# A transformer block on one core: halves at the head, five more rows turned by DMA, means spread through DRAM, all Q/K pairs as seven products

## The chip, the cores and the metric

The kernel runs on one core of a Trainium2 chip. Its engines work side by side, each through its own row of instructions in order: TensorE (PE; its weight loads are listed as PEld), VectorE (DVE), ScalarE (ACT), GpSimd (POOL) and SyncE (SP), whose queue issues all DMAs here. The metric is the device time of one execution in microseconds (us); a kernel's time is the median of its runs.

## The reference, cut to what matters

```python
h  = x + attention(layernorm(x) @ wqkv) @ wo
h2 = h + (gelu(layernorm(h) @ w_gate) * (layernorm(h) @ w_up)) @ w_down
```

x is 2048 x 512, float32. Attention has 32 heads of 16 columns; each position sees eight positions, itself and seven earlier ones at a distance of 2, 4, ... 14, with a softmax over these eight. The feed-forward width is 1792. Layernorm has no learned scale.

## The kernel before

**Tiling.** Four chunks c of 512 tokens, in each four rows j of 128 tokens; 512 columns are four blocks of 128. Tokens are laid on partitions so that the distance of 2 becomes a distance of 1. A float32 product runs as three products in a reduced format: each operand is split into a high part and the rest (`split`: a cast, usually on ScalarE, for `xTh`, `hTh`, `wh`; a subtraction on DVE or POOL for `xTl`, `hTl`, `wl`), and high x high, high x low and low x high are added up. One projection of a row is thus 12 matmuls of 128x512.

**Chunk 0's start.** `WARM` transposes of nothing run on TensorE first (`warm_ps`). `prep0(j)` takes row j's statistics on DVE (`bn_stats`, L585), centres all 512 columns on ScalarE (L587), turns four blocks on TensorE (`tp_x`, L469), and evicts and splits them. `project(c, s, j)` makes k (s=1), q (s=0) or v (s=2); the variance is applied when the sum is evicted.

**Chunks 1 to 3.** x comes transposed from DRAM (`xc`) and is centred there by a tile `mb`, in which the row means lie on every partition: `stats(c)` spreads the means by four TensorE transposes (L629) and a ScalarE copy (L633), for c = 1 and 2. (Chunk 3's x is turned by DMA instead.) `project_pair(c, p)` makes q and k of two rows as seven half-size products in place of eight (L766, into `qka`, `qkb`, `qkc`), with sums of x rows (`sums`: `xS`, `xSl`) and of weights (`weight_sums`: `wsa`, `wsb`, `wT`), which cost DVE and POOL additions and the evictions `qkvt` on DVE (L781). That is 42 matmuls for 48. The pairs in `PLAIN`, here chunk 1's first, take the 48.

**Attention.** `attention(c)` works on four groups of eight heads. k and v go to DRAM and come back shifted (`kw`, `vw`). DVE multiplies (`pk`, L870), reduces (`lg`, L873), multiplies by v (`pv`, L912) and adds up in halves (L917, L919, shared with POOL) to `o_0` to `o_3`. o is turned for the next matmul by DMA (`crossed`: ScalarE copy, DMA transpose, ScalarE copy, then the split) or by TensorE (`tp_o`).

**Tail and feed-forward.** `tail(c)` multiplies by wo (`wo_0` to `wo_3`, one sum per row), adds x (`h`), normalises each row (`norm`: statistics and the last step on DVE, the power on POOL; `xhat_h`) and turns it: by four TensorE transposes `tp_h` with `transpose4`, or, for chunks in `CROSS_H`, by DMA with `crossed` (tile `a_h`). `ffn(c)` runs 14 steps of 128 columns: `pg` and `pu`, the gelu, the product, and `acc` for w_down. Chunks 2 and 3 share one joint feed-forward stage (`last_two`, `joint`, `last_sums`) that again saves products by sums: `combine(j)` makes sums of chunk 2's and 3's hT (`tt`, `tth`, `ttl`) straight from the PSUM bank of `tp_h`, `pa` and `pc` are its accumulators, `jt` their copies on ScalarE.

**Order.** Every operation is added to a plan. `schedule` puts them in order with a list scheduler, which reads one rank per operation from the table `RANKS`; the table `SWAPS` says which operations run on their second engine (DVE or POOL for `either`, ScalarE or DVE for `evict`).

Of the kernel before, what the change touches and what calls it, by code (L numbers as in the profile page):

```python
# [16 lines left out]
P = 128  # L17
D = 512
# [16 lines left out]
WARM = 36  # L35
ONDVE = (1,)
YIELD = 20000
# [6 lines left out]
FINE = (1,)  # L44
FIRST = [("x", 0), (1, 0), (1, 1), ("x", 1), (1, 2), (1, 3), ("x", 2), ("x", 3)] + [(0, k) for k in range(KD)]
# [7 lines left out]
PLAIN = ((1, 0),)  # L53
# [7 lines left out]
CROSS_H = (1, 2)  # L61
RANKS = (
# [186 lines left out]
class Tile:  # L249


    def __init__(self, plan, pool, tag, shape, dtype, name):
        self.make = lambda: pool.tile(shape, dtype, tag=tag, name=name, bufs=1)
        self.ap = None
        self.parts = {}
        self.users = set()
        self.before = plan.slots.get((id(pool), tag))
        plan.slots[id(pool), tag] = self

    def __call__(self):  # L260
# [1282 lines left out]
```

## Time and profile before

| | |
|---|---|
| median of 3 runs | 625.03 us (624.29 to 625.63) |
| profiled execution, its own time | 624.23 us |
| its span, first to last instruction | 622.4 us |
| granted TensorE clock, mean | 1.000 |
| busy: PE, DVE, ACT, POOL | 614.1, 541.4, 426.7, 422.6 us |
| DMA bytes | 153.19 MB, 246 GB/s over the span |

The profile is of one execution. A row of the timeline has its start and length in us, the engine, the source line, the operation, output<-inputs, the shape and how many instructions the row holds; in square brackets stands how long the engine idled before and who released it. A matmul's end is modelled, so that rows on TensorE overlap: the distance of two starts tells the cadence.

### The profile page before, as it was taken

What the parts mean: (1) busy time and instruction counts of PE and PEld (TensorE: products, weight loads), DVE (VectorE), ACT (ScalarE), POOL (GpSimd) and SP (SyncE); (2) the same over time, 40 slices, a digit from 0 to 9 for tenths busy, and PEclk for the clock granted to TensorE, in tenths of its full rate; (3) what the DMA queues carried; (4) which work ended last, traced back from release to release, by engine and by line L of the source; (5) the groups of instructions that cost most, each with busy time, mean ns of one, the idle gap of its engine ahead of it and who ended that gap; (6) DMA issues with size and microseconds to landing.
All of it is one profiled execution on the core that took longest, in us unless ns stands there. A gap on an engine that the chain in (4) does not pass through costs nothing.

```text
span 622.4 us, 8450 instructions
## 1 busy us (share of the span) xinstructions
PE 614.1 (99%) x2728; PEld 503.9 (81%) x2728; DVE 541.4 (87%) x614; ACT 426.7 (69%) x743; POOL 422.6 (68%) x373
## 2 busy tenths in 40 slices
PE   8999999999999999999999999999999999999997
PEld 7888887878888888888888888877768878888885
DVE  4789999898999899999899999979849888768994
ACT  5797587547645666997767767978856666658751
POOL 4999888655899898573577773546475736578751
PEclk9999999999999999999999999999999999999999
DMA  8766688599969887999979897984756555639973
GB/s 299 265 213 250 199 257 265 165 334 309 327 216 323 255 239 225 323 317 355 325 276 314 294 295 214 240 255 108 222 180 216 181 184 194 219 110 309 250 220 102
DMA packets 101084, 153.19 MB, mean 246 GB/s; under 512 B 42016, under 2 KB 55072, under 8 KB 100656
## 3 DMA queue, kind: packets, MB, share of 16 engines
q1 hardware_dynamic: 101040, 152.65, 77.2%
q8 instruction: 21, 0.34, 0.2%
q14 instruction: 23, 0.19, 0.1%
HBM read 107.48 MB, written 36.23 MB: 231 GB/s over the span
## 4 chain that ended last, share of the span: by engine, by line
PE 88%; DMA 4%; DVE 3%; ACT 2%; issue 1%; POOL 1%; SPq 0%; DVEq 0%; ACTq 0%; POOLq 0%
PE pg L544 12%; PE pu L544 12%; PE qkv L544 10%; PE dn L1315 10%; PE pa L1197 8%; PE wo L544 7%; PE pc L1197 5%; PE acc L1006 4%; PE acc L1004 4%; PE acc L1005 4%; PE qka L766 3%; DMA fraw<-in_wffn_dram 2%; PE pg L1419 2%; PE qkv L537 2%; PE pu L1419 1%; PE qkc L766 1%
## 5 line engine op out<-in xcount | busy, mean ns | idle before, releaser
L917 POOL TENSOR_TENSOR pv<-pv 128x1024 f32<-128x1024 f32 (+1 forms) x44 | 84.8, 1931 | 19.5 <-DVE pv L912 18.6
L870 DVE TENSOR_TENSOR pk<-kw,qp 128x2048 f32<-128x2048 f32 x32 | 72.9, 2278 | 1.6 <-ACT qp L863 0.8
L873 DVE TENSOR_REDUCE lg<-pk 128x128 f32<-128x2048 f32 x32 | 72.8, 2278 | 0.5
L912 DVE TENSOR_TENSOR pv<-vw,qp 128x2048 f32<-128x2048 f32 x32 | 72.6, 2281 | 0.6
L544 PE MATMUL pg<-hTh,gu 128*128 128x512 f32 x224 | 59.9, 389 | 0.0
L544 PE MATMUL pu<-hTh,gu 128*128 128x512 f32 x224 | 59.9, 389 | 0.0
L544 PEld LDWEIGHTS pg<-hTh,gu 128*128 128x128 f32 x224 | 42.0, 188 | 8.9 <-ACT hTh L457 0.2
L544 PEld LDWEIGHTS pu<-hTh,gu 128*128 128x128 f32 x224 | 42.0, 188 | 8.7
L1004 PE MATMUL acc<-dnh,gh 128*128 128x512 f32 x112 | 43.6, 389 | 0.0
L1005 PE MATMUL acc<-dnl,gh 128*128 128x512 f32 x112 | 43.6, 389 | 0.0
L1006 PE MATMUL acc<-dnh,gl 128*128 128x512 f32 x112 | 43.6, 389 | 0.0
L458 POOL TENSOR_TENSOR gl<-g,gh 128x512 fp32r<-128x512 f32 x21 | 27.8, 1323 | 9.6 <-ACT gh L457 9.6
L458 POOL TENSOR_TENSOR gu<-fraw,gu 128x512 fp32r<-128x512 f32 x22 | 29.7, 1358 | 6.6 <-ACT gu L457 6.6
L1197 PE MATMUL pa<-tt,jh 128*128 128x512 f32 x112 | 30.3, 392 | 0.3 <-ACT jh L1177 0.3
L544 PE MATMUL pg<-hTl,gu 128*128 128x512 f32 x112 | 30.1, 390 | 0.0
L544 PE MATMUL pu<-hTl,gu 128*128 128x512 f32 x112 | 29.9, 389 | 0.0
L1227 ACT COPY jt<-pa 128x512 f32<-128x512 f32 x32 | 18.7, 586 | 12.4 <-PE pa L1197 6.5
L544 PE MATMUL qkv<-wh,xTh 128*128 128x512 f32 x96 | 25.8, 393 | 0.3 <-ACT qkvt L828 0.3
L917 DVE TENSOR_TENSOR pv<-pv 128x512 f32<-128x512 f32 (+1 forms) x20 | 25.6, 1284 | 0.2
L544 PE MATMUL qkv<-wl,xTh 128*128 128x512 f32 x96 | 25.7, 389 | 0.0
L544 PE MATMUL qkv<-wh,xTl 128*128 128x512 f32 x96 | 25.5, 392 | 0.0
L1197 PEld LDWEIGHTS pa<-tt,jh 128*128 128x128 f32 x112 | 20.8, 188 | 5.6 <-ACT jh L1177 0.9
(479 smaller groups left out, 1842.5 us busy)
## 6 DMA issues: line engine op xcount, KB each, us to landing
fraw<-in_wffn_dram SPq DMA_DIRECT2D x47, 768.0 KB, 5.8
kw<-kv SPq DMA_DIRECT2D x16, 704.0 KB, 6.3
vw<-kv SPq DMA_DIRECT2D x16, 704.0 KB, 5.5
gu<-ld SPq DMA_DIRECT2D x19, 512.0 KB, 4.6
kv<-qkvt SPq DMA_DIRECT2D x32, 256.0 KB, 3.3
ld<-gu SPq DMA_DIRECT2D x14, 512.0 KB, 4.2
ws<-sums_kw SPq DMA_DIRECT2D x21, 256.0 KB, 2.7
x<-in_x_dram SPq DMA_DIRECT2D x16, 256.0 KB, 4.8
```

The lines of the kernel that those rows point to most:

```text
L458: sub = lambda eng: eng.tensor_tensor(lo(), src(), hi().bitcast(F32), op=ALU.subtract)
L544: nc.tensor.matmul(acc(), a, b, start=(p == k == 0 and not seeded), stop=(p == n - 1 and k == KD - 1), skip_group_check=seeded)
L766: nc.tensor.matmul(acc(), a(k), b()[:, k], start=first and q == k == 0, stop=q == 2 and k == 1, skip_group_check=not first)
L870: nc.vector.tensor_tensor(pr(), k4, q2.unsqueeze(2).to_broadcast([P, 2, W, QF]), op=ALU.mult)
L873: dve(2195, lambda pr=pr, jj=jj: nc.vector.tensor_reduce(lg()[:, i, jj:jj + 2], pr().rearrange("p j w (h d) -> p j w h d", d=DH), axis=AX. ...
L912: nc.vector.tensor_tensor(pr().rearrange("p j w (h d) -> p j w h d", d=DH), v5, e5, op=ALU.mult)
L917: either(home, 256 * m, lambda eng, pr=pr, m=m: eng.tensor_tensor(pr()[:, :, 0:m], pr()[:, :, 0:m], pr()[:, :, m:2 * m], op=ALU.add), [], ...
L1004: nc.tensor.matmul(a, gh()[:, sl], dh(), start=(i == 0 and not SEED), stop=False, skip_group_check=SEED)
L1005: nc.tensor.matmul(a, gh()[:, sl], dl(), start=False, stop=False, skip_group_check=SEED)
L1006: nc.tensor.matmul(a, gl()[:, sl], dh(), start=False, stop=(i == NF - 1), skip_group_check=SEED)
L1197: nc.tensor.matmul(acc(), a[:, k], b(k), start=first and p == k == 0, stop=p == 2 and k == 1, skip_group_check=not first)
L1315: nc.tensor.matmul(acc(), a[0]()[:, cols], b[0](), start=first and q == 0, stop=last and q == 2, skip_group_check=True)
```

## The change

- **Head.** `WARM` goes from 36 to 30. For rows 0 and 1 of chunk 0 (`SOON`), `prep0_halves` takes the sum of the first 256 columns on DVE and of the other 256 on ScalarE, adds the two, centres one half on each engine, turns two blocks at a time and evicts the halves on ScalarE and DVE. The statistics follow later, for the variance. The first projection reads the halves as they come. The k weights' casts may run on DVE. x rows 1 and 0 are loaded ahead of the weights.
- **PLAIN** is empty: chunk 1's first pair is made as seven products too.
- **Means.** `stats(c)` for chunks 1 and 2 writes the 512 means to DRAM, 4 bytes a piece, and reads them back spread over 128 partitions as `mb` (256 KB).
- **CROSS_H** names rows instead of chunks: besides all rows of chunks 1 and 2 now rows 0 and 1 of chunk 0 and 0, 1 and 2 of chunk 3. For chunk 3 `combine(j)` reads the turned row in SBUF, and three ScalarE copies go.
- **Order.** `PLACES` holds one start per operation, and `schedule` sorts by it; `SWAPS` is new. DVE's order has 671 operations for 615, POOL's 336 for 376, SP's 425 for 416. TensorE has 2622 matmuls of 128x512 for 2628, and 36 transposes of data for 64.

```diff
-WARM = 36
+WARM = 30
+SOON = (0, 1)
-PLAIN = ((1, 0),)
+PLAIN = ()
-CROSS_H = (1, 2)
+CROSS_H = ((0, 1), (0, 1, 2, 3), (0, 1, 2, 3), (0, 1, 2))
-RANKS = (
-    2221194, 2198587, 2272583, 2916000, 2497537, 2552399, 2552201, 2488295, 2549292, 2863281, 2488296, 2724370, 2867947, 2867946, 2835096, 2465784,
...
+PLACES = (
...
     def schedule(self):
...
+        for o, start in zip(self.ops, PLACES):
+            o.start = start
         return sorted(self.ops, key=lambda o: (o.start, o.n))
...
+        if s == 1:
+            evict(lambda: wh[s]()[:, k], lambda: t()[:, k], [(t, k)], [(wh[s], k)], "ACT", {"ACT": 525, "DVE": 465}, True)
+            either(WLOW[s][k], 512, lambda eng: eng.tensor_tensor(wl[s]()[:, k], t()[:, k], wh[s]()[:, k].bitcast(F32), op=ALU.subtract),
...
+    def prep0_halves(j):
...
+        dve(330, lambda: nc.vector.tensor_reduce(st()[:, 6:7], part(src, 0), axis=AX.X, op=ALU.add), [(src, None)], [(st, "a")])
+        act(430, lambda: nc.scalar.activation(part(xh, 1), part(src, 1), AF.Identity, scale=1.0 / D, accum_out=st()[:, 7:8]),
+            [(src, None)], [(xh, 1), (st, "b")])
+        dve(90, lambda: nc.vector.scalar_tensor_tensor(st()[:, 8:9], st()[:, 6:7], 1.0 / D, st()[:, 7:8], op0=ALU.mult, op1=ALU.add),
+            [(st, "a"), (st, "b")], [(st, "m")])
+        dve(300, lambda: nc.vector.tensor_scalar(part(xh, 0), part(src, 0), st()[:, 8:9], -1.0, op0=ALU.subtract, op1=ALU.mult),
+            [(src, None), (st, "m")], [(xh, 0)], lock=True)
+        act(450, lambda: nc.scalar.activation(part(xh, 1), part(src, 1), AF.Identity, bias=st()[:, 8:9], scale=-1.0),
+            [(src, None), (st, "m")], [(xh, 1)])
...
+        dve(615, lambda: nc.vector.bn_stats(st()[:, 0:6], src()), [(src, None)], [(st, "v")])
...
-        tp = bank("mm1", f"mean_{c}")
...
-        pe(450, spread, [(ident, None), (mv, None)], [(tp, None)])
-        mb = T("ex", [P, D], name=f"mb_{c}")
-        act(490, lambda: nc.scalar.copy(mb(), tp()), [(tp, None)], [(mb, None)])
+        mb, md = T("ex", [P, D], name=f"mb_{c}"), T(f"mean_{c}", [J, P], pool=dram)
+        dma(lambda: md().rearrange("j p -> p j"), lambda: mv()[:, :, 0], 4 << 16, [(mv, None)], [(md, None)])
+        dma(mb, lambda: bass.AP(tensor=md().tensor, offset=md().offset, ap=[[0, P], [1, D]]), 1 << 18, [(md, None)], [(mb, None)])
...
-            if c in CROSS_H:
-                crossed([(xh, None)], xh, lambda j=j: hT_h()[:, :, j], lambda j=j: hT_l()[:, :, j], (hT_h, j), (hT_l, j), f"h_{c}_{j}")
+            if j in CROSS_H[c]:
+                crossed([(xh, None)], xh, lambda j=j: hT_h()[:, :, j], lambda j=j: hT_l()[:, :, j], (hT_h, j), (hT_l, j), f"h_{c}_{j}",
+                        also=combine(j) if c == NC - 1 else None)
```

In the rows below the numbers at the end of a tile's name only tell tiles apart; `tp_x_152<-ident,xhat_x_0_134` turns row 0 of x, `qkv_1_0_187` is k of row 0, x4 is four instructions in a row.

TensorE at the program's start, before:

```order
L444 MATMUL warm_ps<-ident 128x128 x23
L469 MATMUL tp_x_152<-ident,xhat_x_0_134 128x128 x4
L444 MATMUL warm_ps<-ident 128x128 x13
L537 MATMUL qkv_1_0_187<-wh_142,xTh_0_163 128x512 x2
L469 MATMUL tp_x_196<-ident,xhat_x_1_183 128x128 x4
L537 MATMUL qkv_1_0_187<-wh_142,xTh_0_163 128x512 x2
L537 MATMUL qkv_1_0_187<-wl_150,xTh_0_163 128x512 x2
L537 MATMUL qkv_1_1_214<-wh_142,xTh_1_207 128x512
```

and now:

```order
L396 MATMUL warm_ps<-ident 128x128 x22
L559 MATMUL tp_x_139<-ident,xhat_x_1_117 128x128 x2
L396 MATMUL warm_ps<-ident 128x128 x2
L559 MATMUL tp_x_139<-ident,xhat_x_1_117 128x128 x2
L559 MATMUL tp_x_154<-ident,xhat_x_0_130 128x128 x2
L396 MATMUL warm_ps<-ident 128x128 x2
L559 MATMUL tp_x_154<-ident,xhat_x_0_130 128x128 x2
L396 MATMUL warm_ps<-ident 128x128
L491 MATMUL qkv_1_1_173<-wh_147,xTh_1_165 128x512
L396 MATMUL warm_ps<-ident 128x128
L491 MATMUL qkv_1_0_179<-wh_147,xTh_0_169 128x512
```

Both rows are turned, in halves, ahead of the first product; before, row 1 was turned behind two products of row 0.

TensorE from the last o piece's transposes of chunk 0 to its wo, before (`tp_o_3_2` turns half of o_3, `qkc` belongs to chunk 1):

```order
L469 MATMUL tp_o_3_2_1309<-ident,o_3_1279 128x128 x2
L766 MATMUL qkc_1_1314<-wT_281,xS_1_1200 128x512 x4
L766 MATMUL qkc_1_1314<-wT_281,xSl_1_1215 128x512 x2
L766 MATMUL qkc_0_1087<-wh_235,xS_0_1054 128x512 x2
L766 MATMUL qkc_0_1087<-wl_249,xS_0_1054 128x512 x2
L766 MATMUL qkc_0_1087<-wh_235,xS_0_1054 128x512 x2
L766 MATMUL qkc_1_1314<-wh_235,xS_1_1200 128x512 x2
L766 MATMUL qkc_1_1314<-wl_249,xS_1_1200 128x512 x2
L766 MATMUL qkc_1_1314<-wh_235,xS_1_1200 128x512 x2
L544 MATMUL qkv_2_1_1226<-wh_301,xTl_1_1026 128x512 x4
L544 MATMUL wo_0_1360<-wo_h,oTh_912 128x512 x4
```

and now, with the rows that follow:

```order
L421 MATMUL tp_o_3_2_1333<-ident,o_3_1291 128x128 x2
L751 MATMUL qkc_0_1154<-wh_214,xS_0_1066 128x512 x2
L751 MATMUL qkc_0_1154<-wl_254,xS_0_1066 128x512 x2
L751 MATMUL qkc_0_1154<-wh_214,xS_0_1066 128x512 x2
L498 MATMUL wo_1_1349<-wo_h,oTh_1061 128x512 x4
L498 MATMUL wo_0_1361<-wo_h,oTh_1061 128x512 x4
L498 MATMUL wo_0_1361<-wo_l,oTh_1061 128x512 x4
L498 MATMUL wo_0_1361<-wo_h,oTl_1088 128x512 x4
L751 MATMUL qkc_1_1310<-wh_214,xS_1_1240 128x512 x2
L751 MATMUL qkc_1_1310<-wl_254,xS_1_1240 128x512 x2
L751 MATMUL qkc_1_1310<-wh_214,xS_1_1240 128x512 x2
L498 MATMUL wo_1_1349<-wo_l,oTh_1061 128x512 x4
```

Of the 22 products between these transposes and the first wo, six are left.

DVE on its way to the first `pk`, before:

```order
L609 BN_AGGR mvx_348<-st_3_351 128x2
L458 TENSOR_TENSOR wl_362<-wr_157,wh_301 128x512
L704 TENSOR_TENSOR wT_366<-wsb,wT_366 128x1024
L652 TENSOR_TENSOR xc_3_238<-xc_3_238,mb_433 128x512
L870 TENSOR_TENSOR pk_0_0_471<-kw_0_416,qp 128x2048
```

and now:

```order
L689 TENSOR_TENSOR wT_345<-wsb,wT_345 128x1024
L600 BN_AGGR mvx_285<-st_2_343 128x2
L600 BN_AGGR mvx_285<-st_3_352 128x2
L689 TENSOR_TENSOR wT_263<-wsa,wT_263 128x1024
L410 TENSOR_TENSOR wl_341<-wr_137,wh_328 128x512
L689 TENSOR_TENSOR wT_397<-wsa,wT_397 128x1024
L410 TENSOR_TENSOR wl_341<-wr_137,wh_328 128x512
L855 TENSOR_TENSOR pk_0_0_427<-kw_0_370,qp 128x2048
```

Two more weight sums' low parts stand ahead of the first `pk` on DVE, and the subtraction of `mb` has gone behind it.

More of the change, by code (lines that the diff above doesn't have):

```diff
@@ L34 @@
 LAG = 2
-WARM = 36
+WARM = 30
 ONDVE = (1,)
-YIELD = 20000
 PRS = lambda k: f"pr{k % 3}" if k < THREE else ("pr0", "pr1", "pr2", "more")[k % 4]
@@ L60 @@
 CROSS_O = ((0, 1, 2), (0, 1, 2, 3), (0, 1, 2, 3), (0, 1, 2))
-CROSS_H = (1, 2)
-RANKS = (
[167 rows of a table removed]
+CROSS_H = ((0, 1), (0, 1, 2, 3), (0, 1, 2, 3), (0, 1, 2))
+PLACES = (
[154 rows of a table added]
 )
 SWAPS = (
[9 rows of a table removed]
-)
-RATE = 330
-AHEAD = {"DVE": 1000, "POOL": 500}
[10 rows of a table added]
+)
+FAR = ("kv", "k_", "v_", "ld_", "ws_", "hs_", "qd_", "mean_")
 ENGINES = ("PE", "DVE", "ACT", "POOL", "SP")
@@ L256, in __init__ @@
         self.users = set()
+        self.far = tag.startswith(FAR)
         self.before = plan.slots.get((id(pool), tag))
@@ L266 @@
 class Op:
-    __slots__ = ("engine", "busy", "done", "emit", "deps", "next", "rank", "start", "n", "table", "nbytes", "lock", "other")
+    __slots__ = ("engine", "busy", "done", "emit", "deps", "next", "rank", "start", "n", "table", "nbytes", "lock", "late", "other")
 class Plan:
@@ L275, in __init__, with add @@
         self.slots = {}
-    def add(self, engine, busy, emit, reads=(), writes=(), table=None, nbytes=0, lock=False, after=()):
+    def add(self, engine, busy, emit, reads=(), writes=(), table=None, nbytes=0, lock=False, late=2000, after=()):
         o = Op()
-        o.engine, o.busy, o.emit, o.table, o.nbytes, o.lock, o.other = engine, busy, emit, table, nbytes, lock, None
+        o.engine, o.busy, o.emit, o.table, o.nbytes, o.lock, o.late, o.other = engine, busy, emit, table, nbytes, lock, late, None
         o.done = busy + TAIL[engine] + (nbytes / 330 + 2600 if nbytes else 0)
@@ L315, in schedule @@
     def schedule(self):
-        for o, rank in zip(self.ops, RANKS):
-            o.rank = rank
-        ready = {e: [] for e in ENGINES}
-        missing = {o: len(o.deps) for o in self.ops}
-        when = {o: 0.0 for o in self.ops}
-        for o in self.ops:
-            if not missing[o]:
-                ready[o.engine].append(o)
-        free = dict.fromkeys(ENGINES, 0.0)
-        wire, table, lock, holder = 0.0, None, 0.0, None
-        for _ in range(len(self.ops)):
-            at, e = min((max(free[e], min(when[o] for o in ready[e])), e) for e in ENGINES if ready[e])
-            o = max((o for o in ready[e] if when[o] <= at), key=lambda o: (o.rank, -o.n))
-            if e in AHEAD:
-                soon = max((x for x in ready[e] if when[x] <= at + AHEAD[e]), key=lambda x: (x.rank, -x.n))
-                fits = [x for x in ready[e] if max(at, when[x]) + x.busy <= when[soon]]
-                if at < when[soon] < at + o.busy:
-                    o = max(fits, key=lambda x: (x.rank, -x.n)) if fits else soon
-                    at = max(at, when[o])
-            if e == "DVE" and o.lock and holder == "POOL" and lock > at + 250:
-                other = [x for x in ready[e] if when[x] <= at and not x.lock and x.rank > o.rank - YIELD]
-                o = max(other, key=lambda x: (x.rank, -x.n)) if other else o
-            ready[e].remove(o)
-            busy, done = o.busy, o.done
-            if o.table and o.table != table:
-                busy, done, table = busy + 1280, done + 1280, o.table
-            if o.lock:
-                if holder != e:
-                    at = max(at, lock)
-                holder, lock = e, at + busy
-            if o.nbytes:
-                wire = max(wire, at + 1300) + o.nbytes / (250 if at < 8000 else RATE)
-                done = wire - at + 900
-            o.start, free[e] = at, at + busy
-            for x in o.next:
-                same = x.engine == e == "PE"
-                when[x] = max(when[x], at + (busy if same else done))
-                missing[x] -= 1
-                if not missing[x]:
-                    ready[x.engine].append(x)
+        for o, start in zip(self.ops, PLACES):
+            o.start = start
         return sorted(self.ops, key=lambda o: (o.start, o.n))
@@ L408, in either, with evict @@
         return o
-    def evict(dst, src, r, w, home="ACT", ns={"ACT": 490, "DVE": 605}):
+    def evict(dst, src, r, w, home="ACT", ns={"ACT": 490, "DVE": 605}, lock=False):
         away = "DVE" if home == "ACT" else "ACT"
-        o = plan.add(home, ns[home], lambda: nc.scalar.copy(dst(), src()) if o.engine == "ACT" else nc.vector.tensor_copy(dst(), src()), r, w)
+        o = plan.add(home, ns[home], lambda: nc.scalar.copy(dst(), src()) if o.engine == "ACT" else nc.vector.tensor_copy(dst(), src()), r, w, lock=lock)
         o.other = away, ns[away]
@@ L417, in dma @@
     def dma(dst, src, nbytes, r=(), w=(), eng=None, **k):
-        return plan.add("SP", 400, lambda: nc.sync.dma_start(dst(), src()), r, w, nbytes=nbytes, **k)
+        late = 2200 if not r else 1340 if not w or w[0][0].far else 2000
+        return plan.add("SP", 450, lambda: nc.sync.dma_start(dst(), src()), r, w, nbytes=nbytes, late=late, **k)
     kv = T("kv", [2, 2, NQ, PAD + U, QF], pool=dram)
@@ L482, in turn @@
             src, [(tmp, None)])
-        plan.add("SP", 400, lambda: nc.sync.dma_start_transpose(
-            words(flat).rearrange("p (k t) -> p k t", t=P), words(tmp)), [(tmp, None)], src, nbytes=1280 * w)
+        plan.add("SP", 450, lambda: nc.sync.dma_start_transpose(
+            words(flat).rearrange("p (k t) -> p k t", t=P), words(tmp)), [(tmp, None)], src, nbytes=800 * w)
         if into:
@@ L579, in tile_block, with emit @@
     counts["mvx"] = 1
+    def prep0_halves(j):
+        src, st = xts[0, j], ring("st", 3, [P, 16], name=f"st_x0_{j}", pool=tiny)
+        xh = ring("xhat", 2, [P, D], name=f"xhat_x0_{j}")
+        part = lambda t, i: t()[:, i * 2 * P:(i + 1) * 2 * P]
+        dve(330, lambda: nc.vector.tensor_reduce(st()[:, 6:7], part(src, 0), axis=AX.X, op=ALU.add), [(src, None)], [(st, "a")])
[7 more added lines that the diff above has]
+            [(src, None), (st, "m")], [(xh, 1)])
+        h, l = new_xT(0, j)
+        tp = bank(("aux", "mm0")[j % 2], f"tp_x_{j}")
+        for i, home in enumerate(("ACT", "DVE")):
+            def emit(i=i):
+                for k in (2 * i, 2 * i + 1):
+                    nc.tensor.transpose(tp()[:, k * P:(k + 1) * P], xh()[:, k * P:(k + 1) * P], ident())
+            pe(224, emit, [(ident, None), (xh, i)], [(tp, i)])
+            src2 = lambda i=i: part(tp, i).rearrange("p (k t) -> p k t", k=2)
+            hi, lo = (lambda i=i: h()[:, 2 * i:2 * i + 2]), (lambda i=i: l()[:, 2 * i:2 * i + 2])
+            evict(hi, src2, [(tp, i)], [(h, i)], home, {"ACT": 310, "DVE": 340})
+            dve(340, lambda hi=hi, lo=lo, src2=src2: nc.vector.tensor_tensor(lo(), src2(), hi().bitcast(F32), op=ALU.subtract),
+                [(tp, i), (h, i)], [(l, i)])
+        dve(615, lambda: nc.vector.bn_stats(st()[:, 0:6], src()), [(src, None)], [(st, "v")])
+        dve(90, lambda: nc.vector.bn_aggr(mvx0()[:, j, 0:2], st()[:, 0:6]), [(st, "v")], [(mvx0, (j, 0))])
     def prep0(j):
+        if j in SOON:
+            return prep0_halves(j)
         src = xts[0, j]
@@ L624, in stats @@
             return
-        tp = bank("mm1", f"mean_{c}")
-        def spread():
-            for j in range(J):
-                nc.tensor.transpose(tp()[:, j * P:(j + 1) * P], mv()[:, j, 0:1].to_broadcast([P, P]), ident())
-        pe(450, spread, [(ident, None), (mv, None)], [(tp, None)])
-        mb = T("ex", [P, D], name=f"mb_{c}")
-        act(490, lambda: nc.scalar.copy(mb(), tp()), [(tp, None)], [(mb, None)])
+        mb, md = T("ex", [P, D], name=f"mb_{c}"), T(f"mean_{c}", [J, P], pool=dram)
+        dma(lambda: md().rearrange("j p -> p j"), lambda: mv()[:, :, 0], 4 << 16, [(mv, None)], [(md, None)])
+        dma(mb, lambda: bass.AP(tensor=md().tensor, offset=md().offset, ap=[[0, P], [1, D]]), 1 << 18, [(md, None)], [(mb, None)])
         means[c] = (mb, mv)
```

31 lines of the change are left out of this document (21 added, 10 removed), and 339 rows, old and new, of tables (PLACES, RANKS, SWAPS).

## Prediction

> **What bounds the kernel now.** I read the page first: busy times, the slices, the chain that ended last. Then TensorE's waits (engine and line that waits, what it waited for, total us, times, longest), and then the timeline stage by stage.
>
> ```profile
> PE 614.1 (99%) x2728; PEld 503.9 (81%) x2728; DVE 541.4 (87%) x614; ACT 426.7 (69%) x743; POOL 422.6 (68%) x373
> PE   8999999999999999999999999999999999999997
> DVE  4789999898999899999899999979849888768994
> PEclk9999999999999999999999999999999999999999
> PE 88%; DMA 4%; DVE 3%; ACT 2%; issue 1%; POOL 1%; SPq 0%; DVEq 0%; ACTq 0%; POOLq 0%
> ...
> PE pa L1197 <- ACT jt L1227: 1.1, 2, 0.9
> PE tp_h L469 <- DVE mv_h L522: 0.4, 1, 0.4
> ```
>
> TensorE is the chain (88%), it is full in every slice but the first and the last, and its clock is granted in full. Its longest waits behind the head are 0.9 us for jt and 0.4 us for mv_h. So the time is the number of TensorE instructions times their cadence, plus the head before they run dense and the tail behind the last. But VectorE (DVE) is at 9 tenths in most slices of the first two thirds: little can be added to it before TensorE waits for it. The cadence, from the timeline (start, duration, instructions in the row):
>
> ```profile
> 28.07 1.98 PE L544 MATMUL qkv<-wh,xTl 128*128 128x512 f32 x8
> 29.88 1.07 PE L544 MATMUL qkv<-wh,xTh 128*128 128x512 f32 x4
> ...
> 31.69 0.60 PE L629 MATMUL mean<-ident,mvx 128*128 128x128 f32 x4
> 32.05 1.17 PE L544 MATMUL qkv<-wh,xTl 128*128 128x512 f32 x4
> ```
>
> Eight 128x512 products take 29.88 - 28.07 = 1.81 us, 0.2267 each. Four transposes push the next row back by 0.36 us, though the row itself says 0.60, since its end overlaps the next.
>
> **The change part by part.**
>
> TensorE's own work. Pair (1,0) takes 42 products for 48: 6 x 0.2267 = 1.36 us. Two groups of four mean transposes and five groups of four tp_h transposes go: 7 x 0.36 = 2.52 us. Together **-3.9 us**, and TensorE is the bound wherever they stood, so all of it counts unless another engine comes late. The six warm transposes count nothing themselves, because the head ends when data arrive:
>
> ```profile
> 4.87 0.69 DVE L585 BATCH_NORM_STATS2 st_x<-x 128x6 f32<-128x512 f32 x1 [4.02 <-DMA x<-in_x_dram]
> 5.81 0.72 ACT L587 ACTIVATE xhat_x<-x,mvx 128x512 f32<-128x512 f32 x1 [3.60 <-DVE mvx L586]
> 6.44 1.12 ACT L457 CAST wh<-wr 128x512 fp32r<-128x512 f32 x2
> ...
> 1.35 4.86 PE L444 MATMUL warm_ps<-ident 128*128 128x128 f32 x23 [1.35 <-POOL ident masks.py:199]
> 6.59 0.66 PE L469 MATMUL tp_x<-ident,xhat_x 128*128 128x128 f32 x4 [0.38 <-ACT xhat_x L587]
> 7.08 1.58 PE L444 MATMUL warm_ps<-ident 128*128 128x128 f32 x13
> 8.42 0.71 PE L537 MATMUL qkv<-wh,xTh 128*128 128x512 f32 x2
> 9.40 0.66 PE L469 MATMUL tp_x<-ident,xhat_x 128*128 128x128 f32 x4 [0.27 <-ACT xhat_x L587]
> 10.77 0.62 PE L537 MATMUL qkv<-wl,xTh 128*128 128x512 f32 x2
> ```
>
> Head. From the landing of x (4.87) to the first product (8.42) are 3.55 us: statistics, centring, transposes, eviction, 512 columns at each step. In halves, on two engines at once, each step is an estimated half, so some 1.5 us less. But the weights now follow two x rows instead of one; in the trace the SyncE queue issues loads 0.47 us apart (an estimate from its first ones), and the first wh cast, at 6.44 now, moves to about 7. The first product then comes at about 8.0: 0.4 gained. Next, from 8.42 to 10.77 there are 2.35 us that hold four products (0.91) and four transposes (0.36): 1.08 us are gaps, because row 1 is turned there. The new order has rows 0 and 1 turned before the first product, so that most of this goes. Bounds: 0.4 (only the first product is earlier) and 1.5 (all gaps go). I take **-1.2 us**, nearer to the upper end, because both causes are visible rows; the weight loads that come 0.47 later keep the rest.
>
> Attention of chunk 0. This is where the change could cost. DVE's busy time, its first and last rows of the stage with some durations, and the TensorE row that needs its result:
>
> ```profile
> 10.77:36.00 25.23, 25.23 (x118) 20.88 (x117) 18.11 (x23) 19.69 (x39) 23.94 (x16) 1.00 0.83 280
> ...
> sum 89.00, DVE 84.68; mean DVE 21.17
> ...
> 24.81 0.24 DVE L609 BATCH_NORM_AGGREGATE mvx<-st 128x2 f32<-128x6 f32 x2
> 33.02 2.35 DVE L652 TENSOR_TENSOR xc<-xc,mb 128x512 f32<-128x512 f32 x1 [4.13 <-ACT mb L633]
> 36.20 2.29 DVE L870 TENSOR_TENSOR pk<-kw,qp 128x2048 f32<-128x2048 f32 x1 [0.83 <-ACT qp L863]
> 120.82 2.96 DVE L917 TENSOR_TENSOR pv<-pv 128x512 f32<-128x512 f32 x3
> ...
> 106.68 1.42 DVE L917 TENSOR_TENSOR pv<-pv 128x1024 f32<-128x1024 f32 x1
> 110.61 0.69 DVE L458 TENSOR_TENSOR xTl<-xc,xTh 128x512 fp32r<-128x512 f32 x1 [0.48 <-ACT xTh L457]
> 111.22 0.74 DVE L781 SCALAR_TENSOR_TENSOR qkvt<-qkb,mvx,qkvt 128x512 f32<-128x512 f32 x1
> ...
> 125.95 0.38 PE L469 MATMUL tp_o<-ident,o 128*128 128x128 f32 x2
> ```
>
> (The first row is the stretch before attention: behind its length PE, PEld, DVE, ACT, POOL. The second sums four stretches from 36 to 125, DVE alone.) From the first pk to 125 DVE is busy 84.68 of 89.00 us: 4.3 idle. Its rows in the new order that it did not have there: 2 qkvt at 0.74, 6 of 128x512 (wo_l, xTl, 2 xS, 2 xc) at 0.69, 3 of 128x256 at an estimated 0.42, less 3 lg of that size and plus one: 1.5 + 4.1 + 0.4 = 6.0 us. Ahead of the first pk it takes four more 128x1024 products (wsa, wsb, 2 wT) at 1.42, 5.7 us, and in the head two reductions, two centrings, their two combinations, a weight's cast and half a row's, an estimated 2.7 us by halves of the 0.69 rows, less one xc at 2.35: 6.1 us. It has 25.23 - 18.11 = 7.1 us idle there, 4.13 of it waiting for mb, so I hide this.
>
> The last o piece was done at 120.82 + 2.96 = 123.8, 2.2 us before TensorE wanted it (125.95). In the new order 16 products that stood behind that transpose stand ahead of it (+3.6), while 12 products and eight transposes fewer stand ahead of the first wo (3.4) and the head gives 1.2: it is reached at 125.95 + 3.6 - 4.6 = 125.0. If the 6.0 us fill the 4.3 idle first, DVE ends at 125.5 and TensorE waits 0.5 us; if the idle stays, at 129.8, a wait of 4.8; if the rows that POOL no longer runs beside it let DVE run at its undisturbed rate (L652 2.35 here, the 128x512 rows 0.69), nothing. I take **+1.0**, near the row of the filled idle, bounds 0 and +4.8. Chunk 1, whose wo also moves ahead on TensorE by some 42 products, I give **+0.5**, bounds 0 and +4, by the same reading of a DVE that is full.
>
> On why DVE rows stretch, the Trainium skill ("SBUF — State Buffer", "SBUF: two separate sides") says that a DVE instruction with two SBUF inputs and a GpSimd one exclude each other for the whole instruction. The 2.35 us row agrees, 0.69 plus one and a quarter of POOL's 1.3 us instructions. By that rule, work moved from POOL to DVE gives back part of its cost, the wait here would be 0 and the sum 1.0 lower.
>
> The h rows that are turned by DMA. The eight rows that take this way already, with durations min/median/max:
>
> ```profile
> L481 ACT COPY a_h<-xhat_h x8: 1032/1042/1047, 251.1 to 386.3; 128x1024 uint16<-128x1024 uint16 x8
> L487 ACT COPY a_h<-xhat_h x8: 1332/1372/1382, 257.3 to 393.6; 128x1024 uint16<-128x1024 uint16 x8
> L457 ACT CAST hTh<-a_h x8: 613/619/628, 259.1 to 396.3; 128x512 fp32r<-128x512 f32 x8
> L458 DVE TENSOR_TENSOR hTl<-a_h,hTh x3: 676/680/856, 262.1 to 398.3; 128x512 fp32r<-128x512 f32 x3
> DMA to landing us min/median/max: 3.1/3.7/6.0
> ...
> 138.45 1.07 PE L544 MATMUL wo<-wo_h,oTl 128*128 128x512 f32 x4
> 139.94 0.63 PE L469 MATMUL tp_h<-ident,xhat_h 128*128 128x128 f32 x4 [0.42 <-DVE mv_h L522]
> ```
>
> A turn is 1.04 + 3.7 + 1.37 + 0.62 + 0.68 = 7.4 us behind the normalised row; with an estimated 3 us for sum, statistics and normalising (four DVE passes of 0.7), 10.4 behind wo. Between the last product of wo_1 and pg_0 the new order has 48 products and eight transposes, 48 x 0.2267 + 0.72 = 11.6 us. So it is covered by 1.2 us at the median landing and late by 1.1 at the slowest. ScalarE has room (69%). What goes is the wait at tp_h_0: four products from 138.45 end at 139.36, the transposes start at 139.94: **-0.6**. The turns of chunk 3 stand in the joint stage, whose longest wait is that for jt (0.9); three rows less to combine from PSUM may shorten it, three turns on ScalarE may lengthen it: 0, bounds -1 and +2.
>
> Mean by DRAM. Instead of transposes and a 0.57 us copy, two transfers in a row. No row writes 4-byte pieces; the nearest are transfers out and back:
>
> ```profile
> qd<-qkvt SPq DMA_DIRECT2D x12, 256.0 KB, 3.0
> q<-qd SPq DMA_DIRECT2D x12, 256.0 KB, 4.7
> ```
>
> That is 7.7 us for a round trip. All statistics of chunk 1 are ready at 25.05 in the trace of before (the row at 24.81). In the new order one wsa, one wsb, one wT and the head's rows stand ahead of them in addition, three times 1.42 and 2.7 us, part of it in idle time: at 30 to 32. So mb lands at about 39, and TensorE wants the first row of chunk 1 at 42.3 (the row at 32.05 and its 52 products to the end of chunk 0, 43.8, less 0.36 and 1.2), for which POOL and ScalarE need 1.3 + 0.6. Covered by some 1.5 us: 0, bounds 0 and +3. The Trainium skill ("DMA: Bandwidth & Descriptors", "Specifications") puts full rate at 512 bytes a piece and more; these 512 pieces are far under it, which speaks against the part, but no row here shows what it would add.
>
> **Sum.** -3.9 - 1.2 + 1.0 + 0.5 - 0.6 = -4.2 us on the profiled execution's 624.23 (span 622.4): 620.0. The median of the runs, 625.03, is 0.8 above that execution, so I predict **620.8 us**. 0.2%, 1.25 us, is about what a measurement of this kernel can tell from no change.
>
> **Rivals.**
> 1. VectorE becomes the bound (the slower side). Place: tp_o of the last o piece and wo_0, in chunk 0 and again in chunk 1. Price: waits of 4.8 and 4 us for my 1.0 and 0.5: 628.1 with both, 624.6 with the first alone. It decides from the point where the two waits pass 5.7 us together, as the other terms give that much. For it: DVE at 9 tenths and 12 us more rows there. Against: 4.3 + 7.1 us idle in that stretch.
> 2. The waits that stand now vanish too, and the head gives its 1.5: DVE terms 0, jt shorter by 1: 624.23 - 3.9 - 1.5 - 0.6 - 1.0 + 0.8 = 618.0. For it: every order on the engines is new. Against: DVE's load.
> 3. Mean late: mb lands after 40.4, TensorE waits up to 3 us at the start of chunk 1: 623.8. For it: mb's load stands on SyncE behind a wait for the first transfer, with x rows and kv behind it.
> 4. Fewer warm transposes, and TensorE is not at full rate when products begin. The first 23 take 4.86/23 = 0.21 us each, the later 13 1.58/13 = 0.12; 15 products slower by that ratio lose 15 x 0.2267 x 0.74 = 2.5 us: 623.3. Against: 22 still stand in a row at the start. The Trainium skill ("TensorE: Matmul & The Clock Gate", "What's actually happening") has half clock until a window of about 3.4 us was busy; 4.86 us of warm transposes agree, and 22 of them still fill that.
> 5. A turned h row lands late: +1.1, 621.9, inside the range.
>
> **How the numbers follow.** My forecast 0.52 (618.5 to 623), rival 1 0.22, half of it over 626.3 and the rest between no change and faster, rival 2 0.13, rival 3 0.06, rival 4 0.04, rival 5 0.03. Slower by over 0.2%: 0.11 from rival 1 and 0.03 from rivals 1 and 3 together, 0.14. Within 0.2%: 0.06 from rival 1, 0.03 from 3 and 4, 0.04 from the edge of my own, 0.13. Faster 0.73. The range reaches from 616.8, a little under rival 2, to 626.0, between the two prices of rival 1; the forecast's own is 618.5 to 623.
>
> **What would show it.** Right: 2622 products and 36 transposes that do work; first product at 8.0 or before and dense from about 9.5; no wait on TensorE over 1 us between 100 and 160; the DVE row of the last o piece ends at 125 to 126. Wrong: a wait of several us at tp_o or wo of chunk 0 or 1 for DVE; at the first chunk 1 product for xTh behind mb; a first pk far later than 36; first products slower than 0.23 us apart.

## The result, and the profile after

The changed kernel is slower: 635.24 us median of four runs (632.77 to 636.01) against 624.71 for the kernel before (624.29 to 625.63), a ratio of 1.016 with a 95% interval of 1.0128 to 1.0192. The forecast was 620.8, its range ended at 626.0. The profiled execution took 632.77 us, span 631.0. It is the fastest of the four: its mean granted clock is 0.995, that of the others 0.991 or 0.992, so the trace shows the least of what the clock cost.

From the page of the changed kernel: busy times, and the slices of TensorE and of the granted clock.

```profile
PE 613.6 (97%) x2688; PEld 500.9 (79%) x2688; DVE 537.0 (85%) x669; ACT 438.9 (70%) x763; POOL 354.2 (56%) x332
PE   8988999999999999999989999999999999999997
...
PEclk9997999999999999999999999999999999999999
```

TensorE issues 40 instructions fewer and its busy time is nearly what it was (613.6 for 614.1): some of its instructions must have become longer. The fourth slice (47 to 63 us) has a granted clock of 7 tenths, and slices 3 and 4 are no longer full. The waits of TensorE name the same place (engine and line that waits, who ended the wait; total us, times, longest):

```profile
PE qkv L498 <- ACT qkvt L813: 2.9, 2, 2.1
PE qka L751 <- DVE xTl L410: 2.3, 1, 2.3
PE pg L498 <- ACT gu L1019: 1.8, 1, 1.8
...
PE qka L751 <- ACT xTh L409: 0.7, 1, 0.7
```

And the timeline of TensorE there, the first seven-product pair of chunk 1:

```profile
41.06 1.98 PE L498 MATMUL qkv<-wh,xTl 128*128 128x512 f32 x8
43.72 0.73 PE L751 MATMUL qka<-wh,xTh 128*128 128x512 f32 x2 [0.68 <-ACT xTh L409]
44.29 0.63 PE L751 MATMUL qka<-wl,xTh 128*128 128x512 f32 x2
47.20 0.73 PE L751 MATMUL qka<-wh,xTl 128*128 128x512 f32 x2 [2.29 <-DVE xTl L410]
49.99 2.08 PE L498 MATMUL qkv<-wh,xTh 128*128 128x512 f32 x4 [2.06 <-ACT qkvt L813]
51.87 1.91 PE L498 MATMUL qkv<-wl,xTh 128*128 128x512 f32 x4
53.58 1.77 PE L498 MATMUL qkv<-wh,xTh 128*128 128x512 f32 x4
55.18 1.09 PE L498 MATMUL qkv<-wh,xTl 128*128 128x512 f32 x4
```

Three waits, 5.0 us together, and then products at half speed: four take 1.88, 1.71 and 1.60 us from start to start, where four at 0.2267 us take 0.91. Counted against 0.2267 us a product, the stretch from 42.9 to 56.1 loses 8.2 us. The stretches of that time (busy time of PE, PEld, DVE, ACT, POOL, then the granted clock, the DMA share and GB/s) show that it is the clock:

```profile
46.00:48.00 2.00, 0.73 (x2) 0.30 (x2) 1.15 (x1) 1.37 (x4) 2.00 (x2) 1.00 0.69 203
48.00:50.00 2.00, 0.01 (x1) 0.01 (x1) 1.68 (x4) 2.00 (x5) 0.29 (x1) 0.56 0.00 0
50.00:52.00 2.00, 2.00 (x5) 1.62 (x6) 2.00 (x3) 2.00 (x4) 1.16 (x2) 0.50 0.00 0
52.00:54.00 2.00, 2.00 (x6) 1.52 (x5) 2.00 (x3) 1.08 (x3) 2.00 (x4) 0.50 0.05 8
54.00:56.00 2.00, 2.00 (x8) 1.64 (x7) 1.80 (x2) 1.63 (x5) 1.97 (x3) 0.74 0.06 7
56.00:58.00 2.00, 2.00 (x11) 1.63 (x10) 2.00 (x1) 0.31 (x1) 1.92 (x3) 1.00 0.92 230
```

The clock falls to 0.50 and is full again from 56. The DMA engines, at 69% before, move almost nothing for 8 us.

What was late is read backwards, from the centring with `mb` (POOL and DVE) to the SyncE queue. First the timelines of POOL, DVE and ScalarE, then of the queue, then the waits of the queue, then the landing times of all four transfers of the means:

```profile
41.21 1.80 POOL L637 TENSOR_TENSOR xc<-xc,mb 128x512 f32<-128x512 f32 x1 [5.81 <-DMA mb<-mean]
41.17 2.39 DVE L637 TENSOR_TENSOR xc<-xc,mb 128x512 f32<-128x512 f32 x2 [3.69 <-DMA mb<-mean]
43.05 0.62 ACT L409 CAST xTh<-xc 128x512 fp32r<-128x512 f32 x1 [4.38 <-POOL xc L637]
```

```profile
25.86 0.39 SPq L370 DMA_DIRECT2D mean<-mvx  x1
...
37.70 0.33 SPq L370 DMA_DIRECT2D mb<-mean  x1
```

```profile
SPq L370 <- DMA mean<-mvx: 19.4, 2, 10.2
```

```profile
DMA to landing us min/median/max: 3.4/7.3/11.8
```

The write of 512 means is issued at 25.86 and the queue can issue the read at 37.70, 11.8 us later. The queue stands for each of the two writes, 10.2 us the longer time and 9.2 the other, and issues nothing else. The read takes 3.4 and 3.5 us, the writes 11.1 and 11.8 (the median of the four is the mean of the two in the middle, so 11.1 follows). `mb` lands at 41.2. By then POOL has stood 5.8 us and DVE 3.7, with a long reduction queued behind its centring; ScalarE stands 4.4, until 43.05.

The trace's records of single DMA packets tell more of the writes. The packets of 4 bytes run between 29.0 and 30.5 and between 46.2 and 47.0, some 9 ns each; the landings come at 37.6 and 54.7. So some 7 us of each write pass behind its last packet. What passes there is not shown.

### The profile page after: what moved, and what is told of

It reads as the page before. It is cut to its first block, busy times and chain, and to the rows that moved or that the text cites. A ratio compares the mean times of both kernels' runs of the same rounds, so it can differ in the third digit from the quotient of the medians.

```text
span 631.0 us, 8394 instructions
## 1 busy us (share of the span) xinstructions
PE 613.6 (97%) x2688; PEld 500.9 (79%) x2688; DVE 537.0 (85%) x669; ACT 438.9 (70%) x763; POOL 354.2 (56%) x332
## 5 line engine op out<-in xcount | busy, mean ns | idle before, releaser
L902 POOL TENSOR_TENSOR pv<-pv 128x512 f32<-128x512 f32 (+1 forms) x39 | 72.7, 1869 | 30.8 <-DVE pv L897 21.8
L1192 PE MATMUL pa<-tt,jh 128*128 128x512 f32 x112 | 30.5, 394 | 0.7 <-ACT gr_xhat L1217 0.5
L902 DVE TENSOR_TENSOR pv<-pv 128x1024 f32<-128x1024 f32 (+1 forms) x25 | 25.8, 1041 | 0.1
L498 PE MATMUL qkv<-wh,xTh 128*128 128x512 f32 x80 | 22.4, 415 | 2.9 <-ACT qkvt L813 2.9
L498 PEld LDWEIGHTS pg<-hTl,gu 128*128 128x128 f32 x112 | 21.0, 188 | 4.5
L498 PEld LDWEIGHTS pu<-hTl,gu 128*128 128x128 f32 x112 | 21.0, 188 | 4.4
```

The costliest lines, as they stand in the source:

```text
L498: nc.tensor.matmul(acc(), a, b, start=(p == k == 0 and not seeded), stop=(p == n - 1 and k == KD - 1), skip_group_check=seeded)
L902: either(home, 256 * m, lambda eng, pr=pr, m=m: eng.tensor_tensor(pr()[:, :, 0:m], pr()[:, :, 0:m], pr()[:, :, m:2 * m], op=ALU.add), [], ...
L1192: nc.tensor.matmul(acc(), a[:, k], b(k), start=first and p == k == 0, stop=p == 2 and k == 1, skip_group_check=not first)
```

## The experiments

**1. The means of the changed kernel back on TensorE.** Everything else, and the order of all other steps, stays.

```diff
-        mb, md = T("ex", [P, D], name=f"mb_{c}"), T(f"mean_{c}", [J, P], pool=dram)
-        dma(... md <- mv[:, :, 0] ...)
-        dma(mb, ... md, spread over 128 partitions ...)
+        tp = bank("mm1", f"mean_{c}")
+        pe(450, spread, ..., place=SPREAD[c][0])       # four transposes
+        act(490, lambda: nc.scalar.copy(mb(), tp()), ..., place=SPREAD[c][1])
```

> The changed kernel with one part undone: the means of chunks 1 and 2 are spread by four TensorE transposes and a ScalarE copy each, as before the change; all other places are kept. Theory A (the mean's way through DRAM lands late, TensorE waits for xT of chunk 1 and loses its clock): the stretch from 42 to 56 us, where the changed kernel loses about 8 us, closes, the clock stays at 1.00 there, and the time falls by 7 to 9 us, to 626 to 628. Theory B (the new order of VectorE and ScalarE ahead of the first pk is what is late, whatever brings the means): the loss there stays above 4 us and the time stays at 631 to 635.

Measured: 625.97 us (622.5 to 628.95, ten runs), 1.0015 of before (0.9991 to 1.004): 9.3 us of the 10.5 that the change lost come back with this one part. In the profiled execution the three waits are gone and the clock stays full; TensorE's timeline and one stretch:

```profile
44.47 1.07 PE L506 MATMUL qkv<-wh,xTh 128*128 128x512 f32 x4
45.38 0.60 PE L628 MATMUL mean<-ident,mvx 128*128 128x128 f32 x4
```

```profile
48.00:50.00 2.00, 2.00 (x11) 1.65 (x10) 1.62 (x1) 1.91 (x6) 1.97 (x3) 1.00 0.83 287
```

The mean part is thereby shown as the cause of nearly the whole loss. But the kernel is not faster than before either, though its TensorE work is 3.2 us less (the 3.9 without two groups of transposes at 0.36). Its waits say what ate that:

```profile
PE pg L506 <- ACT gu L1033: 1.8, 1, 1.8
...
PE pg L506 <- ACT g L1055: 0.8, 2, 0.5
PE qkv L506 <- ACT qkvt L827: 0.7, 1, 0.7
PE pu L506 <- DVE g L1061: 0.7, 1, 0.7
PE pa L1206 <- ACT gr_xhat L1231: 0.6, 1, 0.6
PE pg L1428 <- ACT m_r L1433: 0.6, 1, 0.6
```

These are single waits, at 70, 216, 226, 279, 319, 435 and 476 us, most of them for a ScalarE step; with one at 287 for a load they cost 6.7 us behind the head. The runs also differ among each other: five, at a mean granted clock of 0.999 to 1.000, took 622.5 to 625.9 us, five, at 0.996 or 0.997, 626.05 to 628.95.

**2. The same transfer in 128 pieces of 16 bytes.** A small ScalarE copy gathers the four means of a partition first, so that the write has a quarter of the pieces; `mb` is then read with a stride.

```diff
+        mc = T(f"mc_{c}", [P, J], pool=tiny)
+        act(200, lambda: nc.scalar.copy(mc(), mv()[:, :, 0]), ...)
-        dma(... [J, P] <- mv[:, :, 0] ...)
+        dma(md, mc, ...)                    # md is [P, J]
```

> The changed kernel, with the means still spread through DRAM, but gathered by a small ScalarE copy first and written in 128 pieces of 16 bytes instead of 512 of 4 bytes; the read of 256 KB stays. Theory A1 (the number of tiny pieces makes the write slow: 11.8 and 11.3 us to landing): the write lands in under 5 us and the time falls by 4 to 8 us, to 627 to 631. Rival A2 (any write to DRAM and the wait of the SyncE queue for it costs this much): the write still lands after 9 us or more and the time stays at 633 to 636.

Measured: 629.8 us (626.62 to 631.73, nine runs), ratio 1.0072 (1.0049 to 1.0096). The landing times of the four mean transfers, and TensorE and POOL at the place:

```profile
DMA to landing us min/median/max: 1.6/3.7/4.8
```

```profile
46.33 1.18 PE L505 MATMUL qkv<-wh,xTh 128*128 128x512 f32 x4 [2.06 <-ACT qkvt L822]
47.35 1.78 PE L505 MATMUL qkv<-wl,xTh 128*128 128x512 f32 x4
```

```profile
36.74 1.55 POOL L646 TENSOR_TENSOR xc<-xc,mb 128x512 f32<-128x512 f32 x1 [1.57 <-DMA mb<-mean]
```

The reads alone have 3.1 and 4.8 us, so the writes took 1.6 and 4.3: the landing time goes with the pieces, (11.8 - 4.3) / 384 or about 20 ns for each piece less. Fewer pieces are larger ones here, so the run doesn't tell their number from their size. By the packet records it is the time behind the last packet that shrinks, from some 7 us to 1.7 and 0.5. Not all comes back, 3.8 us over experiment 1 stay. `mb` is there at 36.7 and POOL still waited 1.57 for it. In experiment 1 it was used at 35.60. The strided rows on POOL are also longer (1.55 us, 1.30 in experiment 1), and the write was issued 1.6 us later than in the changed kernel, at 27.50, behind the ScalarE copy; so this run doesn't separate what made up the 3.8. A single wait of 2.06 us was enough here for the clock to fall: four products take 1.58 us behind it.

**3. and 4. The kernel before with its means through DRAM.** In the first, the list scheduler makes the order anew; in the second, the two transfers stand exactly where the transposes and the copy stood.

```diff
-        pe(450, spread, ...);  act(490, copy mb <- tp)
+        dma(md <- mv[:, :, 0]);  dma(mb <- md)             # 3
+        pe(450, dma_start(md, mv[:, :, 0]), ...);  act(490, dma_start(mb, md), ...)   # 4
```

> The kernel of before with one part of the change done: the means of chunks 1 and 2 go through DRAM in 4-byte pieces. Theory A: mb lands about 14 us after the statistics (25), at about 39 to 41 instead of 33, TensorE wants it at about 41 and 60, so the time rises by 3 to 9 us, to 628 to 634, with a stall and perhaps a clock below 1 behind 43 us. Theory B (the means alone are hidden): within 1 us of 624.7.

Measured: 735.3 us, ratio 1.1756 (1.1717 to 1.1795), a miss. The longest waits are for qkvt (21.2) and for wo (7.8), far behind chunk 1's start, and there are waits of over 1 us in every 100 us of the run: the list scheduler's new order is worse nearly everywhere, and nothing follows on the means except that their transfers again took up to 12.0 us.

> The kernel of before in its own order, instruction by instruction; only the eight transposes and two copies for the means are replaced, each at its place, by the two transfers through DRAM (the run before this one let the list scheduler make a new order, so it said nothing on the part alone). Theory A (the write of 512 pieces takes 9 to 12 us and SyncE stands still behind it): mb of chunk 1 lands near 41 instead of 33, TensorE waits 2 to 6 us between 43 and 60 and perhaps loses its clock: 628 to 636. Theory B (it only costs this much together with the new order): within 2 us of 624.7.

Measured: 644.76 us (four runs), ratio 1.0326 (1.0307 to 1.0346): the part alone costs more here than in the changed kernel, and more than was expected. Its longest waits:

```profile
PE qka L768 <- POOL xS L681: 9.7, 1, 9.7
PE qkv L544 <- ACT xTh L457: 2.7, 1, 2.7
PE qkv L544 <- ACT qkvt L830: 2.4, 1, 2.4
```

The 9.7 us are chunk 2's mean, issued at 52.5 and read at 65.6; the others are chunk 1's. POOL waited 19.8 us for `mb` in two waits. In an order that was made for a copy of 0.57 us, both are uncovered; in the order of the changed kernel chunk 2's is nearly covered, as the next experiment shows.

**5. Chunk 1's mean on TensorE, chunk 2's through DRAM.**

```diff
-        mb, md = ...; dma(...); dma(...)
+        if c == 1: ... four transposes and the copy, as in experiment 1
+        else:      ... the two transfers, as in the changed kernel
```

> The changed kernel with only chunk 1's mean back on TensorE; chunk 2's still goes through DRAM in 4-byte pieces. With both back it was 626.0, with none 635.2. Theory A (the late mb of chunk 1 is the cost: TensorE waits at 44 to 50 us and loses its clock): at least 7 of the 9 us come back, 626 to 628, and the clock stays at 1.00 near 50. Rival B (SyncE standing still for 10 us behind the second write, with the stores of v and the loads of the next kw and vw queued behind it, is the larger part): 629 to 634, with waits between 60 and 100 us.

Measured: 627.7 us (625.47 to 631.14, ten runs), ratio 1.0046 (1.0025 to 1.0068). Of the 9.3 us, chunk 1's mean is 7.5 and chunk 2's 1.7, of which the second is no more than likely, since the intervals of this run and experiment 1 overlap. The queue in this kernel stands as long for chunk 2's:

```profile
36.63 0.44 SPq L378 DMA_DIRECT2D mean<-mvx  x1
...
47.85 0.32 SPq L378 DMA_DIRECT2D mb<-mean  x1
48.27 2.92 SPq L378 DMA_DIRECT2D kv<-qkvt  x2
```

Eleven microseconds again, with nothing issued for ten. But no engine waits for this `mb`, and TensorE's longest wait nearby is 1.2 us, at 55. So the price of the standing queue, without a late mean, is in those 1.7 us.

**6. The clock alone.** The changed kernel with 34 transposes of nothing, 18 in the second wait and 16 in the third; the means stay late.

```diff
+                    if gap and q == 2: fill(18)
...
+                if gap: fill(16)
```

> The changed kernel with 34 transposes of nothing put on TensorE into its two waits in front of chunk 1's first products (18 and 16), and nothing else. It makes no data earlier. Theory A (two waits close together let the clock gate close, and some 14 products run at half rate afterwards): the granted clock stays at 1.00 from 48 to 56 us, the rows at 50 to 55 run at 0.23 us a product instead of 0.45, and the time falls by 2 to 3 us, to 632 to 633. Rival (these products are slow for another reason, or the gate closes anyhow): the time stays at 634 to 636.

Measured: 633.68 us (632.22 to 634.81, four runs), ratio 1.0145 (1.0122 to 1.0168). The clock stays full there, and is lost a little later:

```profile
51.06 1.21 PE L505 MATMUL qkv<-wh,xTh 128*128 128x512 f32 x4 [0.32 <-ACT qkvt L831]
52.11 1.09 PE L505 MATMUL qkv<-wl,xTh 128*128 128x512 f32 x4
...
63.31 0.73 PE L767 MATMUL qka<-wh,xS 128*128 128x512 f32 x2 [1.94 <-ACT qkvt L779]
```

```profile
64.00:66.00 2.00, 2.00 (x7) 1.51 (x6) 0.83 (x1) 1.26 (x4) 1.91 (x3) 0.50 1.04 395
```

A TensorE that is earlier runs into the other engines, which are still late: a new wait of 1.94 us at 61, and the clock at 0.50 behind it. That the fall of the clock follows from idleness is shown by this pair, since filling the gaps alone kept it. As a cure it is worth some 1.5 us, which is inside the two intervals; the delay of POOL, DVE and ScalarE remains.

**7. The single waits of experiment 1.** Three kernels on top of it. The first moves six steps ahead in their engine's order (step: new place in the plan's ns), those for which TensorE waited at 70, 226, 279, 319, 435 and 476 us; the second adds three warm transposes at the head; the third moves two more steps, for the waits at 111 and 215 that the first shows.

```diff
+EARLIER = {334: 67428, 1487: 309655, 1071: 219512, 1383: 271401, 1898: 424503, 2181: 463717}
+        for n, s in EARLIER.items():
+            self.ops[n].start = s
...
-            nc.tensor.transpose(wps()[:, 0:P], ident(), ident())
+            for _ in range(4 if i == 21 else 1):                   # second kernel
...
+           490: 107441, 1047: 207581                               # third kernel
```

> The kernel with the means back on TensorE (626.0), and six operations moved ahead of one or two others on their engine, at the six waits of TensorE over 0.4 us that its trace shows (0.71 at 70, 0.69 at 226, 0.50 at 279, 1.82 at 319, 0.57 at 435, 0.58 at 476 us): an eviction ahead of an exp, a weight's cast ahead of the other half's, a product ahead of a pk, a gelu ahead of a cast, two copies out of PSUM ahead of other casts. Theory A (what the change saves is eaten by single operations that stand wrong in the new order): the waits go, 3 to 5 us less, 621 to 623, faster than before. Rival B (engines are full, and each wait moves to the next operation): other waits of the same size appear and the time stays within 1 us of 626.

> The kernel with the six places moved, and three more warm transposes behind the first 22, where TensorE idles 0.55 us before the first x blocks are turned. Five of ten executions with the means on TensorE showed a mean clock of 0.996 and took 2 to 3 us more than those at 1.000. Theory A (the gate opens late at the head in some executions, because the warm stretch has holes): the clock is 1.000 in all executions and the median 1 to 1.5 us under that of the kernel with the six places. Rival B (the gate closes later on, at a wait inside): no difference over 0.5 us, or what the six places did already.

> The changed kernel with the mean rows spread by TensorE and eight steps moved ahead in their engine's order: the six moved before, and two more, an eviction of chunk 0's own qkvt row ahead of the wait at about 111 us and the ScalarE step of g ahead of the wait at about 215 us. Theory A (the single waits that the new order left behind are what still eats the saved TensorE work, and each one moved away is kept): two waits of 0.4 and 0.8 us less than the kernel with six places, 623.4 less about 1, so 621.5 to 622.5, faster than the kernel before by 0.3 to 0.4%. Theory B (a wait moved away comes back at the next place, because VectorE and ScalarE have the same rows to do in the same time): within 0.7 us of 623.4, no difference from the kernel before.

Measured: 623.43 us (622.01 to 626.9, twelve runs), ratio 0.9993 (0.9977 to 1.001); 624.38 us (622.34 to 628.36, twelve runs), ratio 1.0005 (0.9989 to 1.0022); 623.45 us (621.77 to 625.82, twelve runs), ratio 0.9989 (0.9976 to 1.0001). The longest waits that the six moves left:

```profile
PE pg L509 <- ACT g L1058: 1.1, 2, 0.8
PE pg L509 <- DMA gu<-ld: 0.9, 1, 0.9
PE pa L1209 <- ACT jh L1189: 0.7, 1, 0.7
...
PE qka L768 <- ACT qkvt L778: 0.4, 1, 0.4
```

The waits that were moved went or shrank, but one came at 111, at 475 another step took the place of the first, and those at 215 and 286 grew. All that TensorE loses in the profiled execution is 15.5 us, with the head, as in experiment 1. The median is 2.5 us lower all the same; against the kernel before, measured beside each, it is 0.2%, and the two intervals overlap.

The executions at a granted clock of 0.996 or 0.997 are gone, all twelve have 0.998 or more. In the traces of experiments 2 and 6 a mean of 0.997 is one stretch of 3.4 us at 0.50. So it fits that waits were removed behind which the clock fell in some executions; it is not shown, since none of those five was traced. With the third kernel the loss falls to 14.2 us in the profile, but its median stays: theory B of that run. The warm transposes change nothing, and the low clocks were gone without them, so nothing here points to the head. Nor is the clock all of the spread: the slowest run of the second kernel, 628.36 us, had 1.000. A version with a ninth step, the load behind the wait at 287, has no time: at its new place the load would stand ahead of a TensorE step that it depends on. No version is faster than the kernel before by more than a measurement can tell.

## Why the prediction was wrong, step by step

- **Mean by DRAM (0, bounds 0 and +3): the step that failed.** It is worth 9.3 us (experiment 1). It failed in three places. The round trip was priced at 7.7 us (3.0 out, 4.7 back) from transfers of 256 KB in long rows; it took 15.3 (11.8 + 3.5). The term that was too small is the write: it has 512 pieces of 4 bytes, and experiment 2 shows that the pieces are the reason, though not whether by their number or their size. I had written that no row shows such pieces, but took the nearest row as the price and its size as the bound. The rule that spoke against it (the Trainium skill, "DMA: Bandwidth & Descriptors", "Specifications": full rate only from 512 bytes a piece) was quoted and then given no chance; the trace agrees with its direction. Second, the time of need, 40.4, was that of the first centred row counted back from TensorE. Experiment 1 uses `mb` at 35.6, because POOL and DVE centre the rows in between their long rows, in order. Experiment 2, ready at 36.7, still lost 3.8 us, though some of that may be its strided rows. In the other direction the start was misjudged: the statistics were ready at 25.9 and not at 30 to 32, since the new order has them ahead of the last weight sums (DVE makes wT at 25.75 and 28.60). Third, what follows from a late transfer was left out: five microseconds of waits, another 3 for the clock, then POOL, DVE and ScalarE late for chunk 2.
- **Rival 3** had the mechanism (mean late, xTh behind `mb`) and not the size: 3 us and a chance of 0.06. Its price ended with the wait itself.
- **Rival 4** had the clock in the wrong place. The first products ran at full clock with six warm transposes fewer, and three more changed nothing (experiment 7). The clock was lost at 48. On this the Trainium skill ("TensorE: Matmul & The Clock Gate", "Why this matters for your kernels") asks for no idle gap over some 3 us between products. The trace is stricter: gaps of 0.7, 2.3 and 2.1 us, with four and two products between them, closed it, and one of 2.06 in experiment 2. Yet one of 1.8 (experiment 1, 319 us) left the clock at 1.00.
- **TensorE's own work (-3.9): right as a count.** 2622 products and 36 transposes that do work were issued. Experiment 1, with eight transposes more, keeps 3.2 of it.
- **Head (-1.2): mechanism right, size off.** The first product starts at 8.52 in the changed kernel, 8.42 before, and was expected at 8.0; dense products start at 9.55 instead of 10.77. The gain is about 0.8 us. The first product waited for half an x row (`xTh`), whose cast on ScalarE stood behind that of a weight that had just landed, and the dense ones for the next weight's cast:

```profile
7.58 0.62 ACT L364 CAST wh<-wr 128x512 fp32r<-128x512 f32 x1 [0.16 <-DMA wr<-in_wqkv_dram]
8.11 0.87 ACT L364 CAST xTh<-tp_x 128x256 fp32r<-128x256 f32 x2
8.87 0.62 ACT L364 CAST wh<-wr 128x512 fp32r<-128x512 f32 x1
```

- **VectorE at tp_o and wo (+1.0 and +0.5): mis-sized, it was 0.** From 72 to 214 us TensorE loses nowhere more than 0.3 us in experiment 1, where it isn't late; in the changed kernel it has one wait of 0.3 between 100 and 160, for ScalarE. **Rival 1** fell with it: DVE's busy time sank from 541.4 to 537.0 us, though it has 55 instructions more.
- **tp_h (-0.6): right**, no such wait is left. **Turned h rows (rival 5): not seen** in the waits of the changed kernel over 0.3 us.
- **Not in the sum: ScalarE.** It was called roomy at 69% and each step on it costed at nothing. In experiment 1 most of the new single waits end with a ScalarE step (gu, g, qkvt, m_r, gr_xhat); its busy time rose from 426.7 to 440.1. This is where the 4 us of the other parts went: about 3.2 saved in work and 0.8 in the head, and as much lost in waits: counted from the starts, TensorE loses 3.7 us more behind its first 20 products than in the kernel before. Whether they come from the order or from ScalarE's load was tried in experiment 7 and is not settled: with six steps moved the profiled loss stayed at 15.5 us, with eight it was 14.2. Whether another order holds all of the 4 us stays open.

## What to carry to other kernels

A transfer is priced by its pieces as much as by its bytes: if no row of the trace has pieces like it, the upper bound is open, and a wait on the critical engine must be a rival with a real chance. Ask when the consumers' in-order queues reach the data, not when TensorE would need it at the latest, and what a queue that issues in order holds back while it waits. And add to the price of a wait of about 2 us on a dense TensorE what it may cost behind it in clock.

## What the runs showed of the hardware that was not expected

- 512 pieces of 4 bytes took 11.1 and 11.8 us to land; 128 pieces of 16 bytes, the same bytes, 1.6 and 4.3. Some 7 us of each slow landing passed behind the write's last packet.
- One transfer that waited for another stopped the SyncE queue for ten microseconds, and the DMA share fell to 0.00 to 0.06 behind it from 48 to 56, though in experiment 5 a queue that stood as long cost some 1.7 us.
- The clock fell to 0.50 behind a single idle gap of 2.06 us (experiment 2) and stayed full behind one of 1.8 (experiment 1). In the ten runs of experiment 1 the mean granted clock was 0.996 or 0.997 in five, and all of those were slower than the other five.
